# The softmax sums of the later head pairs move from TensorE to GpSimd in an attention and feed-forward kernel

## The chip, the cores and the metric

One core of a Trainium2 chip runs the whole program. The metric is the device time of one execution in microseconds; the median of several runs is compared. A "pair" below is a pair of attention heads, counted from 0 to 23.

## The reference, cut to what matters

```python
def _attn_ref(q, k, v):                      # each (4, 12, 448, 64)
    scores = scale * np.matmul(q, k.transpose(0, 1, 3, 2))
    scores = np.where(causal_mask, -1000000000.0, scores)
    scores = scores - np.max(scores, axis=-1, keepdims=True)
    attn = np.exp(scores)
    attn = attn / (np.sum(attn, axis=-1, keepdims=True) + 1e-09)
    return np.matmul(attn, v)

def _moe_ref(x, w_in, w_out):                # (1792, 768), (768, 2048), (2048, 768)
    h = x @ w_in
    g = np.maximum(0.01 * h, h)
    return g @ w_out
```

The attention's output, its heads side by side, is x. The two weight matrices come as 64-bit floats, and the kernel rebuilds 32-bit values from their words.

## The kernel before, in words

There are 4 batches of 12 heads; two heads make a pair, so each batch has 6 pairs and there are 24 in all. The 448 keys lie on partitions, in 4 chunks of 128 (the last of 64), and queries lie along the free axis; since the mask is causal, chunk c holds only the queries from 128c on, and the four chunks of a head fill 1,024 columns.

Each pair goes through these steps. Its q and k are loaded by SP (`qk_load`), TensorE turns them so that features lie on partitions and ScalarE copies the result to SBUF (`features`, L376 and L379). TensorE makes the scores and adds the mask (`scores`, L407 and L421). ScalarE copies chunk 0 and VectorE takes the maximum with the other chunks (`softmax`, L442, helper line L236), GpSimd takes the maximum over the partitions with one all-reduce per head (L450), VectorE subtracts it (L456) and ScalarE takes the exponential in place (L463). The exponentials lie in the tile `t`, of which there are three, one pair each. TensorE multiplies them by v (`products`, L474) and ScalarE copies the unnormalised output to `xu` (L480, three buffers).

`finish(u)` runs after every second pair and handles pairs u - 1 and u. It needs the sum of the exponentials over all keys, that is over all partitions and chunks. It makes them with TensorE (`sums`, L494): a matrix of ones times each chunk, four heads into one PSUM tile, 32 matmul records for the four chunks. For the batches 2 and 3 (`b >= ADDS`, with ADDS = 2, so from pair 12 on) VectorE first adds chunk 3 to chunk 2, that to chunk 1 and that to chunk 0 (three instructions per pair, helper line L236, tile `t`), and TensorE sums chunk 0 alone, 8 records. ScalarE copies the sums from PSUM (L506, `sr`), a DMA spreads the four rows over 112 partitions (`sc`), VectorE adds 1e-9 and inverts (L509, L510), a DMA stores the result to DRAM (`scr`), and four DMAs on ScalarE's queue broadcast it to `rb` (two buffers). VectorE multiplies `xu` by it, ScalarE rounds the product to the upper part of x and VectorE makes the rest (the tile `xt`).

The first layer (`layer1`, L548) takes one batch at a time: 16 blocks of 18 matmuls, with w_in in an upper and a lower part. The weights are rebuilt in 16 pieces (`weights_in`, `unpack`: L318, L320, L322, L341 on VectorE, with two copies on ScalarE each). Their staging tile is the same memory as the x of the batches 1 and 3, so these can be written only when all weights are done (batch 1), or when the first layer of batch 1 is done (batch 3). Its result goes through ScalarE (L554, two buffers) and SP to DRAM (`gd`). When attention ends, `switch` frees its memory, and the second layer (`layer2`, L735, seven products of half blocks in place of eight) has w_out rebuilt by the same kind of steps.

The order is made by a planner in Python (`Plan`). Every operation is recorded with its engine, a cost in microseconds, its tiles and a due value. `emit` then lists them: whenever an engine is free it takes, of the operations that could start within 0.1 us, the one with the lowest due value. The due value of a pair's operation is `turn(kind, u)`, that is u plus the entry of the table `LATER`; that of weight piece f is `PIECE[0] + PIECE[1] * f`; the layers' matmuls come after everything that is ready. `SAME` favours matmuls of the same layout as the one before. The order on each engine, and on SP's and ScalarE's DMA queues, is fixed by that list; on the chip each queue runs in order and waits on semaphores.

The change touches `LATER`, `PIECE`, `SAME`, `ADDS` and `finish`.

Of the kernel before, what the change touches and what calls it, by code (L numbers as in the profile page):

```python
# [8 lines left out]
F32 = mybir.dt.float32  # L9
# [3 lines left out]
ACTF = mybir.ActivationFunctionType  # L13
ALU = mybir.AluOpType
# [3 lines left out]


LATER = {  # L20
    "add": 29.11, "load": 31.13, "v": 31.53, "transpose": 32.21, "features": 48.43, "scores": -32.29,
    "chunk 0": 29.53, "max": -47.1, "all max": -30.16, "subtract": -15.76, "exp": 53.37, "products": 26.02,
    "take products": 72.72, "sums": -33.79, "take sums": -26.22, "spread": 12.66, "invert": -79.89, "store": -38.91,
    "broadcast": 59.38, "divide": -36.6, "x hi": 59.99, "x lo": 21.48,
}

EARLY = 8

PIECE = (410.28, -44.38)


SAME = 10.69


class Plan:
# [6 lines left out]

    SPLIT, SAME = 0.15, SAME

# [23 lines left out]
    def emit(self, slack, filler):  # L68
# [18 lines left out]
        def at(i):  # L87
            take = ops[i][6]
            if take is None:
                return ready[i]  # L90
            slots = self.pools[take[0]]
            return max(ready[i], min(slots)[0]) if slots else float("inf")
# [12 lines left out]
        for _ in range(n):  # L105
            t, e = min((max(free.get(e, 0.0), min(at(i) for i in c)), e) for e, c in waiting.items() if c)
            assert t < float("inf")
            i = min((i for i in waiting[e] if at(i) <= t + slack.get(e, 0.0)), 
                    key=lambda i: (ops[i][4] - (self.SAME if e == "PE" and ops[i][9] == split else 0.0), i))
            waiting[e].remove(i)  # L110
# [37 lines left out]
def attention_moe_kernel(  # L148
# [15 lines left out]
    nc = tc.nc  # L164
    w_in, w_out = w_in.bitcast(I32), w_out.bitcast(I32)
    B, H, S, D = q.shape
# [28 lines left out]
    p1 = actx.enter_context(tc.tile_pool(name="p1", bufs=1))  # L195
# [3 lines left out]
    P = Plan()  # L199
# [7 lines left out]
    def turn(kind, u):  # L207
        return u + LATER[kind]

    T = {}  # L210
# [7 lines left out]
    def pe(us, emit, r=(), w=(), prio=0.0, **kw):  # L218
        return P.op("PE", us, emit, r, w, prio, **kw)

    def act(n, emit, r=(), w=(), prio=0.0, us=0.0, **kw):
        return P.op("ACT", us or 0.066 + 0.0008 * n, emit, r, w, prio, **kw)

    def dve(n, emit, r=(), w=(), prio=0.0, rate=1.0, chain=0.0, **kw):

        return P.op("DVE", 0.07 + chain + 0.00104 * n * rate, emit, r, w, prio, **kw)

    def dma(kb, out_, in_, r=(), w=(), prio=0.0, hold=0.62, eng="SP", **kw):

        return P.op(eng, hold, lambda: (nc.sync if eng == "SP" else nc.scalar).dma_start(out=out_(), in_=in_()), r, w, prio, late=max(kb, 20) / 380.0, **kw)  # L230

    def copy(out_, in_, n, r=(), w=(), prio=0.0, **kw):
        return act(n + 55, lambda: nc.scalar.activation(out=out_(), in_=in_(), func=kw.pop("func", ACTF.Copy), **kw), r, w, prio)

    def tt(out_, a, b, op, n, r=(), w=(), prio=0.0, **kw):
        return dve(n, lambda: nc.vector.tensor_tensor(out=out_(), in0=a(), in1=b(), op=op), r, w, prio, **kw)  # L236
# [4 lines left out]
    def new(key, pool, shape, dtype, tag):  # L241
        def f():
            T[key] = pool.tile(shape, dtype, tag=tag, name="_".join(str(x) for x in key))
        return f

    def both(*fs):
        def f():
            for g in fs:
                g()
        return f  # L250
# [11 lines left out]
    ones = p1.tile([128, 32], F32, name="ones")  # L262
# [4 lines left out]
    bigs = lambda key: big[P.slot["tp", key]]  # L267
# [115 lines left out]

    order = sorted(segs)
    NTB, NM = 3, 2
    ADDS = 2
    MERGE = [lambda u: u >= 0, lambda u: u >= 99, lambda u: u >= 99]
    for tag, n, width_ in (("M", NM, S), ("MR", 1, S), ("t", NTB, 1024)):
        for i in range(n):
# [93 lines left out]
    def finish(u):  # L483

        b = u // NP
        heads = range(2 * u - 2, 2 * u + 2)
        sr, sc, rc = ("sr", 0), ("sc", 0), ("rc", 0)
        key = ("tp", ("sums", u))

        def sums():  # L490
            for c in chunks:
                qs, n, bank, col = segs[c]
                for e, g in enumerate(heads):
                    nc.tensor.matmul(out=bigs(key[1])[32 * e:32 * e + 32, qs:S], lhsT=ones, rhs=T["t", g // 2 % NTB][:, g % 2, 512 * bank + col:512 * bank + col + n],  # L494
                                     start=c == 0, stop=c == chunks[-1])


        chunks = order[:1] if b >= ADDS else order
        for w in (u - 1, u) if b >= ADDS else ():
            for c in (2, 1, 0):  # L500
                n = segs[c][1] - 128
                at = lambda c, d, w=w, n=n: T["t", w % NTB][:, :, 512 * segs[c][2] + segs[c][3] + d:512 * segs[c][2] + segs[c][3] + d + n]
                tt(lambda at=at, c=c: at(c, 128), lambda at=at, c=c: at(c, 128), lambda at=at, c=c: at(c + 1, 0), ALU.add, 2 * n,
                   (), [("t", w % NTB, e) for e in range(2)], turn("add", u), chain=0.02)
        pe(0.78 if b >= ADDS else 1.95, sums, ["ones"] + [("t", w % NTB, e) for w in (u - 1, u) for e in range(2)], [key], turn("sums", u), rows=120, cfg=4, take=key)
        act(S + 55, both(new(sr, p1, [128, S], F32, "sr"), lambda: nc.scalar.activation(out=T[sr], in_=bigs(key[1])[:, 0:S], func=ACTF.Copy)),  # L506
            [key], [sr], turn("take sums", u), give=key)
        dma(7, lambda: T[sc], lambda: T[sr][0:97:32, :].rearrange("o (p j) -> o p j", j=16), [sr], [sc], turn("spread", u), 0.68)
        dve(16, lambda: nc.vector.tensor_scalar(out=T[sc], in0=T[sc], scalar1=1e-9, scalar2=None, op0=ALU.add), (), [sc], turn("invert", u))  # L509
        dve(100, both(new(rc, p1, [CP, 16], F32, "rc"), lambda: nc.vector.reciprocal(out=T[rc], in_=T[sc])), [sc], [rc], turn("invert", u))  # L510
        scr = dp.tile([4, S], F32, name=f"scr{u}")
        dma(7, lambda: scr.rearrange("a (p j) -> (a p) j", j=16), lambda: T[rc], [rc], [("scr", u)], turn("store", u))
        slot = (b + 1) % 2
        if u % NP == 1:
            P.op("X", 0.0, new(("xt", b), xp, [128, 2 * NP, S], F32R, f"x{slot}"), w=[("x", slot)], prio=u)
        for w in (u - 1, u):
            p = w % NP
            rb, xu, xc = ("rb", w % 2), ("xu", w % 3), ("xp", b, p)
            for e in range(2):
                a = 2 * (w - u + 1) + e  # L520
                dma(158, lambda rb=rb, e=e: T[rb][64 * e:64 * e + 64, :], lambda a=a: scr[a:a + 1].to_broadcast([64, S]),
                    [("scr", u), rb], [(*rb, e)], turn("broadcast", u), 0.47, eng="ACT")
            x = lambda rb=rb: T[rb]
            tt(x, lambda xu=xu: T[xu], x, ALU.mult, S, [xu, (*rb, 0), (*rb, 1)], [rb], turn("divide", u))
            copy(lambda p=p: T["xt", b][:, p], x, S, [rb, (*rb, 0), (*rb, 1), ("x", slot)], [(*xc, "h")], turn("x hi", u))
            tt(lambda p=p: T["xt", b][:, NP + p], x, lambda p=p: T["xt", b][:, p].bitcast(F32), ALU.subtract, S, [rb, (*rb, 0), (*rb, 1), (*xc, "h"), ("x", slot)], [xc], turn("x lo", u))
# [230 lines left out]

    conv = lambda f: PIECE[0] + PIECE[1] * f
    P.op("X", 0.0, new(("stage",), xp, [128, 2 * NP * S], F32, "x0"), w=[("x", 0)], prio=FIRST)
# [6 lines left out]
    for b in range(B):  # L766
        n0 = len(P.ops)
        for u in range(NP * b, NP * b + NP):
            if u:
                qk_load(u)  # L770
            v_load(u)
            features(u)
            scores(u)
            products(u)
            if u % 2 == 1:
                finish(u)
        attention += range(n0, len(P.ops))
        if b < B - 2:
            layer1(b, lambda f: LAST + 100 * b + f)
# [39 lines left out]
```

## Time and profile before

| | |
|---|---|
| median of 3 runs | 613.22 us (612.17 to 614.36) |
| profiled execution: its own time | 613.63 us |
| profiled execution: span | 611.5 us |
| instructions | 10378 |
| HBM read, written | 61.87 MB, 20.27 MB |

The span goes from the first to the last instruction that was profiled. All times in the profile count from its start. PE is TensorE's matmul, PEld its weight load, DVE is VectorE, ACT is ScalarE, POOL is GpSimd and SP is the engine that issues most DMAs; a name with a q behind it (SPq, ACTq) is that engine's instruction queue. Matmuls are pipelined, so the busy time of PE counts overlaps once, and records of one matmul can be longer than the distance to the next.

### The profile page before, as it was taken

How to read it: one execution, taken by the hardware profiler on the slowest of the kernel's cores; microseconds unless marked ns; L12 is line 12 of the kernel's file. 1: busy time of each engine (PE TensorE's matmuls, PEld its weight loads, DVE VectorE, ACT ScalarE, POOL GpSimd, SP SyncE). 2: the span in 40 equal slices, each digit the busy share in tenths (PEclk: the TensorE clock that was granted, in tenths of full speed). 3: DMA queues.
4: the chain of work that ended last, by engine and by line, in shares of the span. 5: the costliest groups of instructions: out<-in, count | busy, mean ns of one | idle time of the engine just before them, and what ended most of it. 6: DMA issues, size and time to landing. Idle time of an engine off the chain costs nothing.

```text
span 611.5 us, 10378 instructions
## 1 busy us (share of the span) xinstructions
PE 595.1 (97%) x3864; PEld 514.4 (84%) x3864; DVE 445.6 (73%) x899; ACT 292.2 (48%) x478; POOL 81.9 (13%) x54
## 2 busy tenths in 40 slices
PE   8989899999999999999999999999999999999997
PEld 7655576689767676779999999999999999999997
DVE  4899998989678677551466899778857575767655
ACT  3778677655555645432333555545333233323331
POOL 2544323321124242220000000000000000000000
PEclk9989999999999999999999999999999999999999
DMA  8977976848375432312588864113523333333201
GB/s 197 215 174 137 189 184 185 201 127 255 118 154 136 123 86 54 92 36 89 191 284 270 285 205 133 62 46 104 155 70 120 89 116 109 101 95 94 70 31 39
DMA packets 130465, 82.89 MB, mean 136 GB/s; under 512 B 72560, under 2 KB 128368, under 8 KB 130416
## 3 DMA queue, kind: packets, MB, share of 16 engines
q1 hardware_dynamic: 126576, 76.74, 44.6%
q10 hardware_dynamic: 3840, 5.51, 3.3%
q8 instruction: 30, 0.49, 0.4%
q14 instruction: 19, 0.16, 0.1%
HBM read 61.87 MB, written 20.27 MB: 134 GB/s over the span
## 4 chain that ended last, share of the span: by engine, by line
PE 68%; DVE 15%; POOL 4%; ACT 4%; issue 3%; DMA 3%; SPq 1%; ACTq 0%; POOLq 0%; DVEq 0%
PE h L735 31%; PE h L548 28%; POOL MR L450 4%; PE S L407 4%; DVE t L456 3%; DVE M L236 3%; PE big L474 2%; DVE stage L322 2%; DVE stage L320 1%; DMA stage<-in_moe_w_in_dram 1%; PE big L376 1%; DVE wl L341 1%; DMA rb<-scr 1%; SPq L230 1%; PE big L494 1%
## 5 line engine op out<-in xcount | busy, mean ns | idle before, releaser
L548 PE MATMUL h<-xt,wh 128*128 128x448 f32 x768 | 223.1, 371 | 1.8 <-DVE t L456 1.8
L735 PE MATMUL h<-W,r 128*128 128x384 f32 x882 | 164.0, 334 | 0.1
L548 PEld LDWEIGHTS h<-xt,wh 128*128 128x128 f32 x768 | 141.2, 188 | 17.3 <-issue 4.2
L735 PEld LDWEIGHTS h<-W,r 128*128 128x128 f32 x882 | 153.7, 188 | 0.7 <-DVE r L601 0.4
L548 PE MATMUL h<-xt,wl 128*128 128x448 f32 x384 | 140.9, 367 | 0.0
L450 POOL PARTITION_ALL_REDUCE MR<-M x48 | 81.3, 1740 | 181.3 <-DVE M L236 145.5
L548 PEld LDWEIGHTS h<-xt,wl 128*128 128x128 f32 x384 | 72.1, 188 | 6.8
L600 ACT ACTIVATE r<-v 128x512 fp32r<-128x512 f32 x70 | 41.9, 599 | 71.9 <-DVE v L598 71.8
L456 DVE TENSOR_TENSOR t<-S,MR 128x64 f32<-128x64 f32 x192 | 67.8, 414 | 5.8 <-POOL MR L450 5.7
L236 DVE TENSOR_TENSOR M<-S,M 128x320 f32<-128x320 f32 x144 | 49.1, 354 | 30.3 <-ACT M L442 20.2
L601 DVE TENSOR_TENSOR r<-v,r 128x512 fp32r<-128x512 f32 x70 | 47.3, 690 | 28.3 <-ACT r L600 26.6
L554 ACT ACTIVATE h<-h 128x448 f32<-128x448 f32 x64 | 34.6, 541 | 66.3 <-PE h L548 40.1
L735 PE MATMUL h<-xw,r 128*128 128x384 f32 x294 | 61.9, 334 | 0.0
L463 ACT ACTIVATE t<-t 128x1024 f32<-128x1024 f32 x48 | 50.7, 1056 | 22.7 <-DVE t L456 20.0
L407 PE MATMUL S<-kq 64*128 64x448 f32 (+3 forms) x384 | 53.5, 413 | 3.0 <-DVE t L456 3.0
L735 PEld LDWEIGHTS h<-xw,r 128*128 128x128 f32 x294 | 51.9, 188 | 0.0
L407 PEld LDWEIGHTS S<-kq 64*128 64x128 f32 x384 | 32.7, 191 | 21.7 <-issue 10.8
L598 DVE TENSOR_TENSOR v<-A 128x512 f32<-128x512 f32 (+1 forms) x71 | 47.8, 690 | 0.0
L474 PE MATMUL big<-t,v 128*64 128x448 f32 (+3 forms) x384 | 46.0, 385 | 0.2 <-ACT kq L379 0.2
L474 PEld LDWEIGHTS big<-t,v 128*64 128x64 f32 x384 | 25.3, 137 | 20.8 <-issue 11.8
L442 ACT ACTIVATE M<-S 128x896 f32<-128x896 f32 (+1 forms) x27 | 22.1, 832 | 21.6 <-PE S L421 21.6
L600 ACT ACTIVATE r<-A 128x512 fp32r<-128x512 f32 x28 | 17.7, 632 | 30.8 <-PE h L735 30.7
(84 smaller groups left out, 517.5 us busy)
## 6 DMA issues: line engine op xcount, KB each, us to landing
gd<-h SPq DMA_DIRECT2D x64, 224.0 KB, 3.1
A<-gd SPq DMA_DIRECT2D x28, 512.0 KB, 3.9
stage<-in_moe_w_in_dram SPq DMA_DIRECT2D x16, 768.0 KB, 7.2
A<-in_moe_w_out_dram SPq DMA_DIRECT2D x16, 768.0 KB, 5.7
kraw<-in_k_dram SPq DMA_DIRECT2D x24, 224.0 KB, 5.4
qraw<-in_q_dram SPq DMA_DIRECT2D x24, 224.0 KB, 5.0
rb<-scr ACTq DMA_DIRECT2D x48, 112.0 KB, 3.0
v<-in_v_dram SPq DMA_DIRECT2D x48, 96.0 KB, 2.2
```

The source lines that it names most:

```text
L236: return dve(n, lambda: nc.vector.tensor_tensor(out=out_(), in0=a(), in1=b(), op=op), r, w, prio, **kw)
L407: nc.tensor.matmul(out=T["S", u, bank, e][:, col:col + n], lhsT=T[kq][rows, 128 * c:128 * c + 128], rhs=T[kq][rows, S + qs:2 * S], start=c ...
L450: P.op("Pool", 1.52, lambda e=e: nc.gpsimd.partition_all_reduce(T[mr][:, e], T[m][:, e], 128, ReduceOp.max), [(*m, e)], [(*mr, e)], turn(" ...
L456: i = dve(len(es) * n, lambda c=c, qs=qs, n=n, es=es: nc.vector.tensor_tensor(out=T[t][:, cut(es), at(c):at(c) + n], in0=s(c, es), in1=T[m ...
L463: act(1024 + 55, lambda e=e: nc.scalar.activation(out=T[t][:, e], in_=T[t][:, e], func=ACTF.Exp, scale=scale), (), [(*t, e)], turn("exp", u))
L474: nc.tensor.matmul(out=bigs(key[1])[64 * e:64 * e + 64, qs:S], lhsT=T[vv][:, c, e, :], rhs=T["t", u % NTB][:, e, 512 * bank + col:512 * ba ...
L548: nc.tensor.matmul(out=T[key][:, :S], lhsT=T[w, f, 1][:, 128 * c:128 * c + 128], rhs=T["xt", b][:, x, :], start=(c == 0 and j == 0), stop= ...
L554: lambda key=key, g=g: nc.scalar.activation(out=T[g], in_=T[key][:, :S], func=ACTF.Prelu, alpha=0.01)),
L598: nc.vector.tensor_tensor(out=x(), in0=get(terms[0]), in1=get(terms[1]), op=ALU.add if terms[2] > 0 else ALU.subtract)
L600: act(n, lambda: nc.scalar.activation(out=hi(), in_=x(), func=ACTF.Copy), [*rd, *hold], [(out_cell, "h")], prio)
L601: return dve(n, lambda: nc.vector.tensor_tensor(out=lo(), in0=x(), in1=hi().bitcast(F32), op=ALU.subtract), [*rd, (out_cell, "h")], [out_c ...
L735: nc.tensor.matmul(out=T[key][:, :HO], lhsT=g()[:, jj * 128:jj * 128 + 128], rhs=W[:, w * HO:(w + 1) * HO], start=(e == 0 and jj == 0 and ...
```

## The change

From finish(9) on, that is for the pairs 8 to 23, the sums are no longer made on TensorE. VectorE adds the chunks (now also for pairs 8 to 11), and GpSimd adds up the partitions of the joined chunk of each head with an all-reduce. Its result stands in every partition of a part of `t` that is free by then; four DMAs per finish, one for each head, take row 0 and spread it over 28 partitions of `sc`. The matmuls and the copy by ScalarE are left out there. Each add and each sum has the due value of its own pair, not of the second of the two. The tables of due values are replaced as a whole.

```diff
 LATER = {
-    "add": 29.11, "load": 31.13, "v": 31.53, "transpose": 32.21, "features": 48.43, "scores": -32.29,
-    "chunk 0": 29.53, "max": -47.1, "all max": -30.16, "subtract": -15.76, "exp": 53.37, "products": 26.02,
-    "take products": 72.72, "sums": -33.79, "take sums": -26.22, "spread": 12.66, "invert": -79.89, "store": -38.91,
-    "broadcast": 59.38, "divide": -36.6, "x hi": 59.99, "x lo": 21.48,
+    "add": 362.91, "load": 53.58, "v": 54.29, "transpose": 55.63, "features": 8.51, "scores": 10.32,
+    "chunk 0": -13.81, "max": 7.89, "all max": -55.51, "subtract": -33.49, "exp": 43.28, "products": 53.56,
+    "take products": 80.72, "sum all": -34.4, "sums": 31.2, "take sums": -13.17, "spread": 19.03, "invert": -30.74,
+    "store": 5.04, "broadcast": 53.24, "divide": -52.56, "x hi": 53.32, "x lo": 18.2,
 }
-PIECE = (410.28, -44.38)
+PIECE = (498.29, -44.66)
-SAME = 10.69
+SAME = 6.83
...
-    ADDS = 2
+    ADDS = 9
...
-        chunks = order[:1] if b >= ADDS else order
-        for w in (u - 1, u) if b >= ADDS else ():
+        chunks = order[:1] if u >= ADDS else order
+        for w in (u - 1, u) if u >= ADDS else ():
             for c in (2, 1, 0):
...
-                   (), [("t", w % NTB, e) for e in range(2)], turn("add", u), chain=0.02)
-        pe(0.78 if b >= ADDS else 1.95, sums, ...)
-        act(S + 55, both(new(sr, p1, [128, S], F32, "sr"), ...), [key], [sr], turn("take sums", u), give=key)
-        dma(7, lambda: T[sc], lambda: T[sr][0:97:32, :].rearrange("o (p j) -> o p j", j=16), [sr], [sc], turn("spread", u), 0.68)
-        dve(16, ... op0=ALU.add), (), [sc], turn("invert", u))
+                   (), [("t", w % NTB, e) for e in range(2)], turn("add", w), chain=0.02)
+        if u >= ADDS:
+            for w in (u - 1, u):
+                t = ("t", w % NTB)
+                for e in range(2):
+                    P.op("Pool", 3.0, lambda t=t, e=e: nc.gpsimd.partition_all_reduce(T[t][:, e, 512:512 + S], T[t][:, e, 512 - S:512], 128, ReduceOp.add),
+                         (), [(*t, e)], turn("sum all", w))
+                for e in range(2):
+                    i = 2 * (w - u + 1) + e
+                    dma(7, lambda i=i: T[sc][28 * i:28 * i + 28, :], lambda t=t, e=e: T[t][0:1, e, 512:512 + S].rearrange("o (p j) -> o p j", j=16),
+                        [(*t, e), sc], [(sc, i)], turn("spread", u), 0.68)
+        else:
+            pe(1.95, sums, ...)
+            act(S + 55, both(new(sr, p1, [128, S], F32, "sr"), ...), [key], [sr], turn("take sums", u), give=key)
+            dma(7, lambda: T[sc], lambda: T[sr][0:97:32, :].rearrange("o (p j) -> o p j", j=16), [sr], [sc], turn("spread", u), 0.68)
+        dve(16, ... op0=ALU.add), [(sc, i) for i in range(4)], [sc], turn("invert", u))
```

## Rows read from the trace of the kernel before

**Rows 1.** The page: busy time and share by engine; granted clock in 40 slices.

```profile
PE 595.1 (97%) x3864; PEld 514.4 (84%) x3864; DVE 445.6 (73%) x899; ACT 292.2 (48%) x478; POOL 81.9 (13%) x54
...
PEclk9989999999999999999999999999999999999999
```

**Rows 2.** Stretches: length, busy PE, PEld, DVE, ACT, POOL, granted clock, DMA share, GB/s.

```profile
12.00:63.00 51.00, 46.17 (x491) 30.06 (x493) 44.83 (x117) 38.92 (x58) 24.07 (x14) 0.97 0.86 191
63.00:156.00 93.00, 88.96 (x655) 69.10 (x652) 86.16 (x174) 57.68 (x80) 26.39 (x15) 1.00 0.72 184
...
164.00:271.00 107.00, 106.39 (x758) 77.55 (x758) 75.16 (x190) 54.72 (x84) 29.16 (x18) 1.00 0.40 103
...
393.00:404.00 11.00, 11.00 (x55) 10.02 (x54) 6.83 (x14) 4.62 (x12) 0.00 (x0) 1.00 0.17 63
```

**Rows 3.** The chain that ended last, in order of time: start, length, what.

```profile
176.16 1.58 PE big L494 x8
...
214.97 1.25 PE big L494 x6
...
239.90 1.74 PE big L494 x8
...
258.23 0.89 PE big L494 x8
...
271.46 129.55 PE h L548 x626
...
419.00 189.23 PE h L735 x1090
```

**Rows 4.** Timeline of TensorE from 92 us: start, length, engine, line, operation.

```profile
93.44 1.93 PE L494 MATMUL big<-t,ones 128*32 128x448 f32 x32
95.31 1.89 PE L474 MATMUL big<-t,v 128*64 128x448 f32 x14
```

**Rows 5.** Groups of VectorE by form: names, shape, count; busy us, mean ns; idle before.

```profile
L236 DVE TENSOR_TENSOR t<-t 128x640 f32<-128x640 f32 x12 | 9.8, 816 | 0.2
...
L236 DVE TENSOR_TENSOR t<-t 128x384 f32<-128x384 f32 x12 | 6.7, 557 | 0.4
...
L236 DVE TENSOR_TENSOR t<-t 128x128 f32<-128x128 f32 x12 | 5.0, 418 | 3.2 <-PE big L474 3.2
```

**Rows 6.** Lines 450 and 322: ns min/median/max, first and last start.

```profile
L450 POOL PARTITION_ALL_REDUCE MR<-M x48: 1604/1682/2392, 11.9 to 262.1; - x48
...
L322 DVE SCALAR_TENSOR_TENSOR stage<-stage x16: 948/958/1722, 24.0 to 153.2; 128x768 int32<-128x768 int32 x16
```

**Rows 7.** Timelines of VectorE and GpSimd near 117 us.

```profile
117.32 1.72 DVE L322 SCALAR_TENSOR_TENSOR stage<-stage 128x768 int32<-128x768 int32 x1 [0.76 <-ACT stage L233]
...
115.71 3.19 POOL L450 PARTITION_ALL_REDUCE MR<-M  x2 [6.89 <-DVE M L236]
```

**Rows 8.** Timeline of VectorE: the last weight piece; the fourth pair's x.

```profile
155.34 0.95 DVE L341 TENSOR_TENSOR wl<-stage,wh 128x768 fp32r<-128x768 f32 x1
...
166.03 0.63 DVE L236 TENSOR_TENSOR xt<-rb,xt 128x448 fp32r<-128x448 f32 x1 [1.34 <-ACT xt L233]
```

**Rows 9.** The first layer's matmuls (line 548) in a stretch: busy PE, PEld.

```profile
156.00:167.00 11.00, 8.99 (x43) 7.59 (x42) 1.00 0.36 121
```

**Rows 10.** Timeline of TensorE: the next batch's first matmuls.

```profile
173.58 0.64 PE L548 MATMUL h<-xt,wh 128*128 128x448 f32 x2
```

**Rows 11.** Timelines of VectorE, ScalarE's queue and SP's queue at the end of attention.

```profile
273.97 0.18 DVE L509 TENSOR_SCALAR sc<-sc 112x16 f32<-112x16 f32 x1 [3.67 <-DMA sc<-sr]
...
292.35 2.39 ACTq L230 DMA_DIRECT2D rb<-scr  x4
...
299.56 0.81 SPq L230 DMA_DIRECT2D A<-in_moe_w_out_dram  x2
```

**Rows 12.** Instructions on the tile sr: ns min/median/max, first and last start.

```profile
L506 ACT ACTIVATE sr<-big x12: 522/544/552, 28.1 to 271.6; 128x448 f32<-128x448 f32 x12
L230 SPq DMA_DIRECT2D sc<-sr x12: 570/604/677, 29.4 to 272.1; - x12
```

More of the change, by code (lines that the diff above doesn't have):

```diff
@@ L503, in finish @@
                 tt(lambda at=at, c=c: at(c, 128), lambda at=at, c=c: at(c, 128), lambda at=at, c=c: at(c + 1, 0), ALU.add, 2 * n,
-                   (), [("t", w % NTB, e) for e in range(2)], turn("add", u), chain=0.02)
-        pe(0.78 if b >= ADDS else 1.95, sums, ["ones"] + [("t", w % NTB, e) for w in (u - 1, u) for e in range(2)], [key], turn("sums", u), rows=120, cfg=4, take=key)
-        act(S + 55, both(new(sr, p1, [128, S], F32, "sr"), lambda: nc.scalar.activation(out=T[sr], in_=bigs(key[1])[:, 0:S], func=ACTF.Copy)),
-            [key], [sr], turn("take sums", u), give=key)
@@ L508, in finish @@
-        dma(7, lambda: T[sc], lambda: T[sr][0:97:32, :].rearrange("o (p j) -> o p j", j=16), [sr], [sc], turn("spread", u), 0.68)
-        dve(16, lambda: nc.vector.tensor_scalar(out=T[sc], in0=T[sc], scalar1=1e-9, scalar2=None, op0=ALU.add), (), [sc], turn("invert", u))
+                   (), [("t", w % NTB, e) for e in range(2)], turn("add", w), chain=0.02)
[10 more added lines that the diff above has]
+        else:
+            pe(1.95, sums, ["ones"] + [("t", w % NTB, e) for w in (u - 1, u) for e in range(2)], [key], turn("sums", u), rows=120, cfg=4, take=key)
+            act(S + 55, both(new(sr, p1, [128, S], F32, "sr"), lambda: nc.scalar.activation(out=T[sr], in_=bigs(key[1])[:, 0:S], func=ACTF.Copy)),
+                [key], [sr], turn("take sums", u), give=key)
+            dma(7, lambda: T[sc], lambda: T[sr][0:97:32, :].rearrange("o (p j) -> o p j", j=16), [sr], [sc], turn("spread", u), 0.68)
@@ L510, in finish @@
+        dve(16, lambda: nc.vector.tensor_scalar(out=T[sc], in0=T[sc], scalar1=1e-9, scalar2=None, op0=ALU.add), [(sc, i) for i in range(4)], [sc], turn("invert", u))
         dve(100, both(new(rc, p1, [CP, 16], F32, "rc"), lambda: nc.vector.reciprocal(out=T[rc], in_=T[sc])), [sc], [rc], turn("invert", u))
```

## The prediction

> **What bounds the kernel now.** I read the page's shares first, then the busy time by stretch, then the chain that ended last, then the rows of the operations that the diff touches. TensorE is busy for 97% of the span, VectorE for 73%, GpSimd for 13% [rows 1]; the granted clock is at full speed nearly throughout, with a dip worth 3% of the stretch from 12 to 63 us [rows 1, 2]. By stretch: up to 156 us VectorE is busy for 88% and more, and TensorE shows 4.8 and 4.0 us of idle time; from 164 to 271 us TensorE shows 0.6 us in 107, while VectorE has 32 us free and GpSimd 78 [rows 2]. The chain ends in 626 matmuls of the first layer in 129.6 us and 1090 of the second in 189.2 us, back to back [rows 3]. So from 164 us on the time is the sum of TensorE's work, and an instruction taken off TensorE there shortens the run by its length; before 156 us VectorE, which also rebuilds the weights, is the tighter engine.
>
> **TensorE: the sums that go.** The finishes of pairs 9 and 11 lose full sums of 32 matmuls. One runs from 93.44 us to the next instruction's start at 95.31: 1.87 us, two are 3.7 us [rows 4]. The six later finishes lose sums of 8 matmuls. In the chain they hold 1.58, 1.25, 1.74 and, three times, 0.89 us: 7.2 us [rows 3]. Six by the shortest would be 5.3; the 1.9 us above that are waits for VectorE's adds, which no TensorE instruction would wait for any more, though another wait may show in their place. Bounds 5.3 and 7.2; I take the middle, **6.3 us**, because TensorE has next work ready in most of this stretch.
>
> **The early sums and the new adds.** Pairs 8 to 11 get three adds each: 0.418 + 0.557 + 0.816 = 1.79 us [rows 5], four pairs 7.2 us of VectorE. Their eight GpSimd sums also stand in VectorE's way. Beside an all-reduce a VectorE instruction with two SBUF inputs took 1.72 instead of 0.96 us, a wait of 0.76 while the second of two all-reduces ran that took 3.19 together [rows 6, 7]. Eight such waits are 6.1 us; that is the upper end, the lower is none: VectorE gets 7.2 to 13.3 us more before the weights are done. What covers it: the last weight is written at 156.3 us, and TensorE still has 43 matmuls of the first layer queued until 167; the fourth pair's x that the next batch needs is written at 166.7, and its matmuls start at 173.6 [rows 8 to 10]. So x may come 6.9 us later for nothing, and TensorE would lose between 0.3 and 6.4 us after that. Against it stand the 3.7 us saved: between 3.4 gained and 2.7 lost. The middle is near nothing, and I take **0** for these two finishes.
>
> The Trainium skill (SBUF — State Buffer, section "SBUF: two separate sides") says that VectorE and GpSimd share a port pair under an exclusive lock held for the full instruction, and counts a VectorE instruction with two SBUF inputs among those that need it. The trace agrees that the two block each other, but with 0.76 us for a lock that would by the page have lasted the rest of that all-reduce, some 1.6 us. By the row the sum above stands; by the page it would be the fourth rival's.
>
> **GpSimd.** The trace has no all-reduce that adds. From below its price is the fastest maximum of the same shape, 1.60 us; the slowest took 2.39 [rows 6]. The planner's costs are 3.0 for it and 1.52 for the maximum, whose median by the trace is 1.68; scaled by that ratio the sum would last 3.3, the upper end. I take 3.0, nearer that end, because the planner's cost is the only one given for this operation. 32 of them are 96 us. In the late stretch nine pairs (18 all-reduces) take 107 us [rows 2], 23.8 us for two pairs; GpSimd needs 4 x 1.68 + 4 x 3.0 = 18.7 us of that. It stays off the path, with 5 us to spare, but no longer idle: a maximum may now queue behind a sum, and the subtraction behind it. The three buffers of exponentials are held longer, by some 6 us of sums and the transfer.
>
> **The last finish.** The sum of a pair ends 6 us (12, if both pairs' sums come last) after its adds, where it was a matmul and a copy. In the trace the last sums reach VectorE at 274.0 us, and the last four broadcasts are issued at 292.4, since they wait for buffers that the first layer frees [rows 11]. Some 18 us lie between; up to 12 us later costs nothing. If that cover is gone, the second layer's weights, whose loads start at 299.6 [rows 11], come later.
>
> **Queues and ScalarE.** Eight copies of 0.54 us leave ScalarE (4.3 us, busy 48%: nothing) [rows 1, 12]. SP gets four spreads of 0.60 us for one, 24 more issues and 14.5 us in all [rows 12]. They now wait for GpSimd; behind them on SP stand the loads of q, k and v and the stores of the first layer's result, whose two buffers TensorE's output waits for. Lower end nothing, upper end 8 x 1.8 us, each finish's three extra issues falling on a store that TensorE waits for. I take nothing: one such block of matmuls lasts 3.7 us (18 of the chain's matmuls at 0.207), longer than the extra issues, and a second buffer stands behind it.
>
> **The order.** All due times move, and every wait of the pairs with them. Bounds: the visible idle time of 9.5 us after 12 us could go, or as much be added [rows 2]. I take nothing.
>
> **Sum.** 6.3 + 0 = 6.3 us off. On the profiled execution (span 611.5, own time 613.6) that gives 605.2 and 607.3; its own time stands 0.4 above the median, so 613.2 - 6.3 = **606.9 us**.
>
> **The rivals.**
> *One: all of it counts.* The early sums lie on TensorE's path too, because layer one ends only at 167 us: 3.7 + 7.2 = 10.9 us off, 602.3. For it: TensorE is 96% busy from 63 to 156 us. Against: VectorE is as full there.
> *Two: VectorE takes the early stretch.* The upper end of its term, 2.7 us lost: 613.2 - 6.3 + 2.7 = 609.6.
> *Three, slower: GpSimd becomes the bound.* Place: the late stretch. It decides from the sum's duration at which 4 x 1.68 + 4d passes 23.8 us, d = 4.3 us. At 5.0 us each of six finishes comes 2.9 us later than the one before allows, 17.6 us at the end. The switch to the second layer waits for it; of that VectorE's idle 4.2 us between 393 and 404 us are the cover [rows 2]. The second layer starts 13.4 us later than before, 626.6. For it: GpSimd and VectorE lengthen each other (1.60 to 2.39 us). Against: 3.0 and 0.8 on top are 3.8.
> *Four, slower: a GpSimd sum holds VectorE's two-input instructions for its whole length.* Eight early sums of 3.0 us, half of it met: 12 + 7.2 - 6.9 = 12.3 lost, less 3.7 and 6.3: 615.5. This is the time by the lock that the Trainium skill's SBUF — State Buffer, "SBUF: two separate sides", describes. The 0.76 us of the trace speak against it.
> *Five: the order gives it back.* Sums queued before maxima, SP behind spreads: new waits of 6 us, two thirds of the bound above, make it 613, with as much chance above as below.
>
> **The numbers.** Forecast (604.5 to 609) 0.41, one 0.18, two 0.14, three 0.09, four 0.04, five 0.14 (0.10 within 0.3%, 0.02 and 0.02 beyond on each side). A measurement of this kernel tells 0.3%, 1.8 us, from no change. Of two, 0.02 ends within it. Faster: 0.41 + 0.18 + 0.12 + 0.02 = 0.73; same: 0.12; slower: 0.15. The range reaches from rival one's 602.0 to 613.5, which leaves out three, four, the upper side of five and a little below.
>
> **What would show it.** Right: no 8- or 32-matmul sums on TensorE after 80 us; 80 all-reduces in place of 48, the new ones near 3 us; the block of first-layer matmuls that ended at 401.0 us ending near 394.7 [rows 3]; TensorE's idle time from 164 us on still below 2 us; attention's last x near 299 us. Early step wrong if x of pairs 6 to 9 is written after 174 us and TensorE waits for it. Wrong altogether: sums of 4.3 us and more with GpSimd busy throughout from 164 us, ScalarE's results waiting for stores behind spreads on SP, or VectorE's idle time before 404 us gone and second-layer matmuls waiting for weights.

## The result and the profile after

The changed kernel took 618.67 us in the median of four executions against 612.82 us of the kernel before on the same chip: a ratio of 1.0087 (95% interval 1.0059 to 1.0114), slower by less than 1%, but clear of noise, where 606.9 us and a range of 602.0 to 613.5 us were forecast. One of the four, the one first profiled, took 1149 us with the same instructions and longer matmuls; the ratio leaves it out (the other three have a median of 618.5 us), and the profile below is that of a further run (e1) whose median is 619.05 us (ratio 1.0114, 1.0081 to 1.0146) and whose profiled execution took 619.43 us, with a span of 617.5 us.

The page of the kernel after, parts 1, 2 and 4: busy time by engine, the granted clock in 40 slices, and the shares of the chain that ended last.

```profile
PE 591.9 (96%) x3748; PEld 512.2 (83%) x3748; DVE 478.0 (77%) x911; ACT 287.9 (47%) x470; POOL 176.4 (29%) x86
...
PEclk9999999899989999999999999999999999999999
...
PE 65%; DVE 19%; POOL 5%; issue 5%; ACT 3%; DMA 2%; SPq 1%; ACTq 0%; POOLq 0%; DVEq 0%
```

Beside [rows 1], 116 matmul records are gone: the 112 of the sums (two finishes of 32, six of 8), as the change says, and four of another line (306). TensorE's busy time fell by only 3.2 us and the span rose by 6.0, so it waits more; in the chain VectorE has 19% (15% before). VectorE's busy time rose by 32.4 us. Its twelve added instructions account for 7.2 of these by [rows 5]; some 25 us are left, in which the same instructions take longer.

Windows of the kernel after: length, busy PE, PEld, DVE, ACT, POOL with their counts, granted clock, DMA share, GB/s.

```profile
12.00:63.00 51.00, 46.81 (x481) 30.23 (x483) 43.18 (x113) 37.99 (x57) 23.34 (x14) 0.97 0.86 185
63.00:156.00 93.00, 85.13 (x562) 65.22 (x558) 89.42 (x162) 52.92 (x78) 40.35 (x19) 0.98 0.72 189
100.00:120.00 20.00, 16.38 (x87) 13.53 (x87) 19.32 (x29) 9.97 (x14) 10.71 (x5) 0.91 0.65 168
164.00:180.00 16.00, 13.23 (x87) 8.63 (x85) 13.56 (x32) 6.80 (x12) 9.42 (x5) 0.89 0.34 92
164.00:271.00 107.00, 101.70 (x696) 76.40 (x695) 86.04 (x188) 50.56 (x76) 85.28 (x38) 0.98 0.38 100
393.00:404.00 11.00, 11.00 (x55) 10.00 (x54) 10.39 (x21) 6.17 (x14) 0.00 (x0) 1.00 0.16 58
```

Against [rows 2], the first and the last row show TensorE as before. Its idle time grows from 4.0 to 7.9 us in the second row's stretch, and from 0.6 to 5.3 us between 164 and 271 us, where the forecast said that it would stay below 2 us. GpSimd is idle for 21.7 us of those 107, so it is not the bound. VectorE is busy for 86 us of them, 11 more than before. The granted clock also falls in two new places, from 100 to 120 us and from 164 to 180 us. TensorE has two levels, 2.4 and 1.2 GHz, and a mean of 0.91 over 20 us is 3.6 us at the lower one. In both stretches TensorE was short of work first (16.38 busy of 20, 13.23 of 16): from 112 to 114 us it was busy for 0.67 us at a granted clock of 1.00, and from 116 to 118 the clock was 0.50; from 170 to 172 it was busy for 0.45 us, and from 174 to 176 the clock was 0.50.

The chain of waits of the kernel after, around the end of the first layer (start, length, what).

```profile
399.96 9.51 PE h L559 x46
409.46 10.58 PE h L746 x61
```

The first layer ends at 409.5 us. In the kernel before its last matmul ended at 403.7; the block of [rows 3] ends at 401.0 because the chain leaves TensorE there. So it ends 5.8 us later, nearly the whole loss, where the forecast wanted that block to end 6.3 us earlier. The second layer follows it without a gap.

### The profile page after: what moved, and what is told of

The parts are those of the page before. It is cut to its first block, busy times and chain, and to the rows that moved or that the text cites. A ratio compares the mean times of both kernels' runs of the same rounds, so it can differ in the third digit from the quotient of the medians.

```text
span 1147.4 us, 10264 instructions
## 1 busy us (share of the span) xinstructions
PE 1142.1 (100%) x3748; PEld 814.0 (71%) x3748; DVE 474.9 (41%) x911; ACT 283.6 (25%) x470; POOL 176.3 (15%) x86
## 4 chain that ended last, share of the span: by engine, by line
PE 99%; DVE 0%; ACT 0%; issue 0%
PE h L559 41%; PE h L746 36%; PE S L407 8%; PE big L474 8%; PE big L376 3%; PE big L494 1%; PE S L421 1%; PE big L306 1%; DVE place L276 0%; DVE ob L760 0%; ACT C L757 0%; PE big L278 0%; DVE row L279 0%; DVE warmb L270 0%; DVE ones L239 0%
## 5 line engine op out<-in xcount | busy, mean ns | idle before, releaser
L559 PE MATMUL h<-xt,wh 128*128 128x448 f32 x768 | 394.9, 615 | 0.0
L746 PE MATMUL h<-W,r 128*128 128x384 f32 x882 | 323.0, 556 | 0.0
L746 PEld LDWEIGHTS h<-W,r 128*128 128x128 f32 x882 | 263.2, 300 | 46.0 <-issue 31.3
L559 PEld LDWEIGHTS h<-xt,wh 128*128 128x128 f32 x768 | 220.1, 292 | 83.3 <-issue 69.2
L559 PE MATMUL h<-xt,wl 128*128 128x448 f32 x384 | 235.1, 612 | 0.0
L559 PEld LDWEIGHTS h<-xt,wl 128*128 128x128 f32 x384 | 112.6, 293 | 41.6 <-issue 35.2
L746 PE MATMUL h<-xw,r 128*128 128x384 f32 x294 | 117.2, 558 | 0.6 <-ACT C L757 0.6
L565 ACT ACTIVATE h<-h 128x448 f32<-128x448 f32 x64 | 34.9, 545 | 303.1 <-issue 162.4
L509 POOL PARTITION_ALL_REDUCE t<-t x32 | 95.0, 3014 | 55.4 <-DVE t L236 28.1
L407 PE MATMUL S<-kq 64*128 64x448 f32 (+3 forms) x384 | 94.9, 655 | 0.0
L474 PE MATMUL big<-t,v 128*64 128x448 f32 (+3 forms) x384 | 92.3, 672 | 0.0
```

What stands on the lines that cost most here:

```text
L407: nc.tensor.matmul(out=T["S", u, bank, e][:, col:col + n], lhsT=T[kq][rows, 128 * c:128 * c + 128], rhs=T[kq][rows, S + qs:2 * S], start=c ...
L474: nc.tensor.matmul(out=bigs(key[1])[64 * e:64 * e + 64, qs:S], lhsT=T[vv][:, c, e, :], rhs=T["t", u % NTB][:, e, 512 * bank + col:512 * ba ...
L509: P.op("Pool", 3.0, lambda t=t, e=e: nc.gpsimd.partition_all_reduce(T[t][:, e, 512:512 + S], T[t][:, e, 512 - S:512], 128, ReduceOp.add), ...
L559: nc.tensor.matmul(out=T[key][:, :S], lhsT=T[w, f, 1][:, 128 * c:128 * c + 128], rhs=T["xt", b][:, x, :], start=(c == 0 and j == 0), stop= ...
L746: nc.tensor.matmul(out=T[key][:, :HO], lhsT=g()[:, jj * 128:jj * 128 + 128], rhs=W[:, w * HO:(w + 1) * HO], start=(e == 0 and jj == 0 and ...
```

## Where the time went

The line of the new all-reduce in the kernel after: ns min/median/max, first and last start.

```profile
L509 POOL PARTITION_ALL_REDUCE t<-t x32: 2873/2952/3432, 104.0 to 294.8; - x32
```

A sum lasts 2.95 us, beside the 1.68 us of a maximum in [rows 6]. The forecast took 3.0 us. Its length was not the error.

Groups of VectorE by form, of the kernel after: names, shape, count; busy us, mean ns; idle before.

```profile
L322 DVE SCALAR_TENSOR_TENSOR stage<-stage 128x768 int32<-128x768 int32 x16 | 19.3, 1204 | 0.7 <-ACT stage L233 0.3
...
L236 DVE TENSOR_TENSOR t<-t 128x384 f32<-128x384 f32 x16 | 16.6, 1035 | 0.5
L236 DVE TENSOR_TENSOR t<-t 128x640 f32<-128x640 f32 x16 | 15.5, 969 | 0.6
L236 DVE TENSOR_TENSOR t<-t 128x128 f32<-128x128 f32 x16 | 6.0, 378 | 2.4 <-PE big L474 2.4
```

The weight step of line 322 has a median of 0.958 us in both kernels [rows 6]; its mean was 1.04 and is now 1.20. Of the adds, which took 0.816, 0.557 and 0.418 us [rows 5], the one of 384 columns now has nearly double its time and is the longest, although the one of 640 has more to do: what was added is waiting, not work.

Two instructions of VectorE, and what GpSimd did beside them, in the timelines of the kernel after (start, length, engine, line, operation; in brackets the idle time before).

```profile
111.10 2.19 DVE L318 TENSOR_SCALAR stage<-stage 128x768 int32<-128x768 int32 x1
...
119.27 2.67 DVE L322 SCALAR_TENSOR_TENSOR stage<-stage 128x768 int32<-128x768 int32 x1 [0.27 <-ACT stage L233]
```

```profile
110.83 3.06 POOL L509 PARTITION_ALL_REDUCE t<-t  x1
...
119.17 5.82 POOL L509 PARTITION_ALL_REDUCE t<-t  x2 [5.28 <-DVE t L236]
```

Line 322 starts 0.10 us after the first of two sums and ends 2.77 us after the sum began. Less its own 0.96 us it was held for 1.71, until 1.81 us into the sum: neither the 0.76 us of [rows 7] nor the whole 2.91 us. Line 318, which has one input in SBUF, is held in the same way: it takes 0.55 us when alone (at 121.62 us in the kernel before), and here it ends 2.46 us after the sum before that began, which puts the end of its hold at 1.91 us. The subtractions of line 456, which read one input from PSUM, show no hold: the longest of 192 took 0.62 us.

Counted in this way, as an instruction's length less its length alone, the eight sums of the pairs 8 to 11 held eight instructions, by 0.58, 1.64, 1.71, 0.65, 1.66, 1.87, 0.43 and 0.89 us: 9.4 us. All 32 sums come to some 22 us. The holds beside the maxima rose as well, from 4 to 9 us, but they stay as high in e5 below, which loses nothing.

So the weights come late. The first layer's matmuls with the lower part of the weights in the kernel after (busy us, mean ns; idle time of TensorE before them, and what ended it), and three moments in the timelines of VectorE and of TensorE:

```profile
L559 PE MATMUL h<-xt,wl 128*128 128x448 f32 x384 | 142.1, 370 | 3.8 <-DVE wl L341 3.8
```

```profile
161.41 0.95 DVE L341 TENSOR_TENSOR wl<-stage,wh 128x768 fp32r<-128x768 f32 x1
...
174.51 0.64 DVE L236 TENSOR_TENSOR xt<-rb,xt 128x448 fp32r<-128x448 f32 x1
```

```profile
178.67 0.64 PE L559 MATMUL h<-xt,wh 128*128 128x448 f32 x2
```

In the kernel before these matmuls waited for no weight piece at all. Now TensorE waits three times for the lower part of one, 3.8 us in all, 2.54 of them before 115.21 us. The last piece is written at 162.4 us (156.3 before), the fourth pair's x at 175.2 (166.7) [rows 8]. The matmuls at 178.67 (173.58 before [rows 10]) are the last three of the first batch, since 285 of its 288 come before them. The next batch starts behind them, at 179.35 us (175.30): 4.0 us later, though 3.7 us of sums have left TensorE by then.

## The experiments

Theories, by the letters that the expectations use. **A**: TensorE is short of work and its clock falls. **B**: the replaced order costs the time. **C**: GpSimd's sums hold VectorE's instructions whose inputs all lie in SBUF. **D**: the time that GpSimd needs for a sum makes what waits for it late. **E**: the adds, the spreads or the order that came with the sums cost it.

**e1, the change again.** No edit; for its profile.

> The changed kernel, unedited, for a profile at full clock. All theories: 618.5 us (617.5 to 619.5). Theory A, TensorE runs short of work and its clock falls: mean granted clock 0.989 to 0.994, at least two dips of 3 us or more to the lower level where the kernel before had one, TensorE's idle time outside the dips up by 5 us or more. Theory B, the replaced order delays x: the first matmul of the second batch's first layer starts after 180 us (before 173.6). Theory C, GpSimd's sums hold up VectorE: VectorE's instructions with two SBUF inputs that meet a sum last 1.5 us longer and more, together over 15 us.

619.05 us. The loss stands, with the profile shown above. C's sign is there (some 22 us beside sums, line 318's among them), and so is A's, two new falls of the clock; B's is not, since the second batch starts at 179.35 us, not after 180.

**e2, the new order alone, and e3, the sums in the old order.** Is it B?

```diff
 # e2: the kernel before with the new LATER, PIECE, SAME
 # e3: the changed kernel with the old ones
+    "sum all": -9.05,
```

> The kernel before with the changed tables of due values; the sums stay on TensorE as before. Theory B, the order is what costs: 616 us or more. Theories A and C, it is the sums on GpSimd: within 2 us of the kernel before, 611 to 615.

> The changed kernel with the due values of the kernel before; the new sums get -9.05, 21 behind the maximum, as in the change. Theory B: 608 us or less, the order was at fault. Theories A and C: 617 us or more, since the sums themselves hold up VectorE or starve TensorE whatever the order.

e2 took 614.8 us (1.0040, 1.0014 to 1.0066) and e3 631.9 us (1.0318, 1.0287 to 1.0349). With the sums on TensorE the new order costs 2.6 us (the kernel before took 612.2 beside it); with them on GpSimd it saves 13 against the old one. B falls: the order relieves what the sums do.

**e4, from pair 12 on.** Only the pairs whose weights are done by then should be left.

```diff
-    ADDS = 9
+    ADDS = 13
```

> The changed kernel with the new sums from pair 12 on only; pairs 8 to 11 have their full sums on TensorE as before and no adds. If the loss lies in the early stretch (VectorE full of weights): 610 us or less. If it lies in the later one: 616 us or more.

618.33 us (1.0089, 1.0055 to 1.0123), no gain, which by the expectation puts the loss into the later stretch. But the timelines of VectorE and GpSimd of this kernel, and its window from 180 to 271 us, show another order:

```profile
156.70 2.59 DVE L320 SCALAR_TENSOR_TENSOR stage<-stage 128x768 int32<-128x768 int32 x1
159.39 2.75 DVE L322 SCALAR_TENSOR_TENSOR stage<-stage 128x768 int32<-128x768 int32 x1
...
163.72 0.95 DVE L341 TENSOR_TENSOR wl<-stage,wh 128x768 fp32r<-128x768 f32 x1
```

```profile
156.36 5.89 POOL L509 PARTITION_ALL_REDUCE t<-t  x2 [10.06 <-DVE t L236]
```

```profile
180.00:271.00 91.00, 84.14 (x568) 63.45 (x567) 72.72 (x145) 40.43 (x60) 70.33 (x30) 0.98 0.36 95
```

The planner made the order anew, and put the first two sums beside the rebuilding of the last weight pieces; the last was written at 164.7 us. TensorE's idle time from 180 to 271 us is 6.9 us here and 2.5 in the change, with the same late sums. One edit changed two things, so this run tells nothing apart. From here on the operation was replaced and the order kept.

**e5, e6, e7: something else in the place of each sum, order kept.** One memset of the same tile (no reading, short), six memsets (no reading, as long as a sum), a maximum (reading, shorter). The sums themselves are left out.

```diff
-partition_all_reduce(T[t][:, e, 512:512 + S], T[t][:, e, 512 - S:512], 128, ReduceOp.add)
+nc.gpsimd.memset(T[t][:, e, 512:512 + S], 100.0)                           # e5
+[nc.gpsimd.memset(T[t][:, e, 512:512 + S], 100.0) for _ in range(6)]       # e6
+partition_all_reduce(T[t][:, e, 512:512 + S], T[t][:, e, 512 - S:512], 128, ReduceOp.max)  # e7
```

> The changed kernel with every one of the 32 sums on GpSimd replaced by one memset of the same output; order, adds, spreads and waits are the same (the sums are left out). Theory C, the sums hold up VectorE's two-input instructions: 606 to 610 us, VectorE's instructions with two SBUF inputs back to their own length beside them. Theory D, the sums come late on GpSimd and what waits for them is late: the same, 606 to 610. Theory E, it is the adds, the four spreads and the order, not the operation on GpSimd: 616 us or more.

> The same with six memsets in place of each sum, so that GpSimd is busy for about as long as with the sum (estimate from a memset of 128 columns at 0.2 us: 2.5 to 3.5 us) but reads nothing (the sums are left out). Theory C: 606 to 611 us, since no instruction of VectorE is held. Theory D, GpSimd's time itself: 616 us or more.

> The changed kernel with a maximum in place of each sum, same order (the sums are left out). A maximum lasts 1.7 us and held VectorE 0.8 to 0.9 us, a sum lasts 3.0 and held it 1.8 to 1.9. Theories C and D: between the change and the run with one memset, 610 to 615 us. Theory E: 616 us or more.

e5 took 603.6 us (0.9837, 0.9790 to 0.9884), e6 606.3 (nine executions, a tenth took 613.9; 0.9900, 0.9868 to 0.9933), e7 606.3 (0.9890, 0.9838 to 0.9942). All three beat the kernel before, though each has the adds, the spreads and the order of the change: E falls. e5 is 2 us below what was expected of it and e7 4 us. The instruction that is held at 119.27 us in the kernel after, in the timelines of VectorE and GpSimd of e5:

```profile
115.04 0.96 DVE L322 SCALAR_TENSOR_TENSOR stage<-stage 128x768 int32<-128x768 int32 x1 [0.25 <-ACT stage L233]
```

```profile
114.91 0.89 POOL L509 MEMSET t<- 128x448 f32 x2 [6.24 <-DVE t L236]
```

and of e6:

```profile
117.15 0.96 DVE L322 SCALAR_TENSOR_TENSOR stage<-stage 128x768 int32<-128x768 int32 x1 [0.26 <-ACT stage L233]
```

```profile
117.01 6.78 POOL L509 MEMSET t<- 128x448 f32 x12 [3.31 <-DVE t L236]
```

and in e7, with the row of its maxima in line 509:

```profile
116.15 1.66 DVE L322 SCALAR_TENSOR_TENSOR stage<-stage 128x768 int32<-128x768 int32 x1 [0.26 <-ACT stage L233]
```

```profile
L509 POOL PARTITION_ALL_REDUCE t<-t x32: 1602/1681/2162, 102.9 to 281.7; - x32
```

Beside memsets it takes its 0.96 us, beside a maximum 1.66, beside a sum 2.67. In e6 GpSimd is at work for 3.39 us per head, longer than with a sum, and this instruction is not held; that costs 2 to 3 us against e5. D can have about that much. The sums cost 15.4 (619.0 less 603.6), so C has some 12. A is a consequence: in e5's profile the granted clock is 1.00 between 63 and 300 us, where TensorE waits less (in e14, the same kernel again, it is 0.99, with one fall there). Over the whole kernel the page gives VectorE 478.0 us busy in the kernel after, 457.6 in e5 and 453.6 in e6: 20 to 24 us of holds.

The cost does not go by the length of a hold alone. With maxima VectorE is busy for 463.0 us, a quarter of the way from e5 to the change, and the time is 2.7 us above e5, a sixth of the sums' cost: short holds are mostly covered. One rival is not tested by itself: without the sums x has other values. That e5 and e7, which divide by very different numbers (100 and a maximum), are both fast speaks against it.

**e9, e10: which sums?** Memsets for the sums of pairs 8 to 11 alone (e9), or of pairs 12 to 23 alone (e10); the order is that of the change.

```diff
+(nc.gpsimd.memset(...) if u < 13 else partition_all_reduce(...))     # e9
+(nc.gpsimd.memset(...) if u >= 13 else partition_all_reduce(...))    # e10
```

> The changed kernel with the eight sums of pairs 8 to 11 replaced by one memset each, same order (these sums are left out); pairs 12 to 23 keep theirs. All 32 left out gave 603.6 us, none 619. Theory C1, the holds cost time only where VectorE is full of weights: 606 us or less. Theory C2, they cost in both stretches, and by the ends of the first layer's batches (11 of 15 us lost by the end of the first batch) mostly early: 608 to 612. Theory C3, mostly late: 614 or more.

> The reverse: the 24 sums of pairs 12 to 23 replaced by one memset each, those of pairs 8 to 11 kept. C1: 616 us or more. C2: 610 to 615. C3: 608 or less.

e9 took 610.4 us (0.9958, 0.9939 to 0.9977), e10 611.3 (0.9978, 0.9957 to 1.0000): both as C2 has it.

**e13 to e16: the same kernels again.** A reading of the windows stood in the way: in e9's profile the first layer's matmuls lay further apart than in e10's, 4 to 5 us over the layer, which would have changed the division. No edits: e13 is the kernel before, e14 is e5, e15 is e9, e16 is e10.

> The kernel before, a second profile. Execution (the spacing of the first layer's matmuls varies from execution to execution): 292 or 298 of them between 320 and 380 us, either. Kernel (it belongs to the program): 292 or 293 again, and a time near 612.7.

> The change with each sum replaced by one memset, a second profile. Execution: 292 or 298 matmuls of the first layer between 320 and 380 us, and executions about 4.8 us apart, 603 to 608. Kernel: 298 again, 603.6 again.

> The change with the sums of pairs 8 to 11 replaced by memsets, a second profile. Execution: 292 or 298 matmuls between 320 and 380 us, median near 610.4. Kernel: 292 again; then 4.8 of the 6.8 us between this kernel and the one without sums are the spacing, and the late sums cost 2 to 3 us, not 7.8.

> The change with the sums of pairs 12 to 23 replaced by memsets, a second profile. Execution: 292 or 298 matmuls between 320 and 380 us, median near 611.3. Kernel: 297 or 298 again; then the early sums cost 7.7 us at equal spacing, as before.

The window from 320 to 380 us (columns as above), of e9 and, the same kernel, e15:

```profile
320.00:380.00 60.00, 60.00 (x292) 54.49 (x292) 49.66 (x79) 29.06 (x53) 0.00 (x0) 1.00 0.75 246
```

```profile
320.00:380.00 60.00, 60.00 (x298) 55.61 (x297) 48.76 (x76) 28.07 (x52) 0.00 (x0) 1.00 0.74 239
```

and of e10 and, the same kernel, e16:

```profile
320.00:380.00 60.00, 60.00 (x297) 55.61 (x297) 50.68 (x80) 29.86 (x53) 0.00 (x0) 1.00 0.75 251
```

```profile
320.00:380.00 60.00, 60.00 (x292) 54.50 (x291) 48.86 (x75) 29.08 (x51) 0.00 (x0) 1.00 0.78 256
```

292 matmuls became 298, and 297 became 292: the spacing belongs to the single execution, so medians of several executions may be compared, and spans of two profiles only to within 5 us. The kernel before, run beside each set of experiments, had medians of 612.1 to 612.8 us, so sets may be put together. e13 took 612.4 us (0.9998, 0.9979 to 1.0016), e14 604.8 (0.9882, 0.9845 to 0.9919), e15 609.4 (0.9949, 0.9925 to 0.9973), e16 613.2 (1.0018, 0.9999 to 1.0037).

The medians over both sets of each kernel: no sums 604.1 (8 executions), the late ones alone 609.9 (19), the early ones alone 612.5 (20), all of them 618.7 (7, the change's own included). The eight early sums thus cost 8.4 us (612.5 - 604.1) or 8.8 (618.7 - 609.9), the 24 late ones 5.8 or 6.2, whichever is taken first; together they are the 14.6 us. Resampling the executions leaves 1 to 2 us of doubt on each side of these four. Per sum an early one costs some four times as much as a late one. The windows show where. The kernel before, before and after the last weight piece:

```profile
100.00:165.00 65.00, 61.58 (x407) 50.81 (x404) 57.66 (x106) 40.24 (x57) 14.20 (x8) 1.00 0.62 173
...
180.00:271.00 91.00, 90.47 (x644) 66.58 (x642) 64.10 (x166) 46.28 (x68) 25.75 (x16) 1.00 0.35 94
```

Without sums, in the order of the change (e5):

```profile
100.00:165.00 65.00, 61.00 (x367) 49.36 (x365) 59.51 (x106) 38.60 (x57) 14.39 (x15) 1.00 0.63 180
...
180.00:271.00 91.00, 90.54 (x622) 69.25 (x621) 67.85 (x164) 44.71 (x67) 34.20 (x34) 1.00 0.34 93
```

With the early sums alone (e10):

```profile
100.00:165.00 65.00, 57.03 (x318) 45.91 (x313) 63.10 (x96) 33.09 (x49) 29.91 (x13) 0.97 0.58 168
...
180.00:271.00 91.00, 90.43 (x621) 69.36 (x619) 66.47 (x161) 45.65 (x67) 34.12 (x34) 1.00 0.40 104
```

With the late sums alone (e9):

```profile
100.00:165.00 65.00, 60.59 (x367) 49.48 (x365) 58.59 (x103) 38.67 (x56) 13.77 (x14) 1.00 0.64 182
...
180.00:271.00 91.00, 88.11 (x608) 66.43 (x608) 70.04 (x158) 44.08 (x64) 75.97 (x34) 1.00 0.34 93
```

Early, against e5: VectorE does 96 instructions where it did 106, in 3.6 us more; it is busy for 63 of 65 us, TensorE loses 4.0 us of busy time and the clock falls to 0.97. From 100 to 180 us TensorE is idle for 10.0 us in e10 and 8.9 in e16, against 4.2 and 4.3 in e5 and e14: 5.2 more. The granted clock over these 80 us is 0.96 and 0.94 instead of 1.00, which is 3.2 and 4.8 us. An estimate from these rows is thus 5.2 of waiting and some 4 of clock, near the 8.4 to 8.8 measured; no run separates the two.

Late: VectorE has 21 us free in 91 and TensorE is yet idle for 2.9 us instead of 0.5. Free time on VectorE does not cover a hold there, because each engine takes its instructions in order, and behind the held one stand steps that others wait for. The longest of these waits, in the timelines of GpSimd, VectorE, ScalarE and TensorE of e9:

```profile
196.18 5.96 POOL L509 PARTITION_ALL_REDUCE t<-t  x2 [3.38 <-issue]
```

```profile
194.29 5.12 DVE L236 TENSOR_TENSOR t<-t 128x128 f32<-128x128 f32 x6
```

```profile
201.81 0.58 ACT L233 ACTIVATE xt<-rb 128x448 fp32r<-128x448 f32 x1 [1.03 <-DVE rb L236]
202.29 0.53 ACT L480 ACTIVATE xu<-big 128x448 f32<-128x448 f32 x1
```

```profile
202.87 0.60 PE L376 MATMUL big<-ident,qraw 112*128 112x112 f32 x4 [1.11 <-ACT xu L480]
```

The same in e5, VectorE, ScalarE and TensorE:

```profile
191.50 3.39 DVE L236 TENSOR_TENSOR t<-t 128x128 f32<-128x128 f32 x6
```

```profile
198.17 0.58 ACT L233 ACTIVATE xt<-rb 128x448 fp32r<-128x448 f32 x1 [0.18 <-DVE rb L236]
```

```profile
199.23 0.60 PE L376 MATMUL big<-ident,qraw 112*128 112x112 f32 x4 [0.26 <-ACT xu L480]
```

A sum holds one of the six adds, so they take 5.12 us instead of 3.39. VectorE's multiplication into `rb` comes later, ScalarE waits 1.03 us for it instead of 0.18, and its copy to `xu`, which TensorE's line 376 waits for, stands behind. Part of the late cost can be D: in e6, with no sum to hold VectorE, TensorE is idle for 1.7 us of the same 91. No run separates the two there.

**e8, e11, e12: sums on GpSimd only where VectorE has no weights to rebuild.** Based on the kernel before and its order; from pair 18 (e8), 16 (e11) or 14 (e12) on, TensorE's sums as before up to there.

```diff
+    "sum all": -9.05,
-    ADDS = 2
+    ADDS, ALL = 13, 19        # e11: 17, e12: 15
...
+        if u >= ALL:
+            ...               # GpSimd's sums, as in the change
+        else:
+            pe(0.78 if u >= ADDS else 1.95, sums, ...)
```

> The kernel before with its own due values, and the sums on GpSimd for pairs 18 to 23 only (three finishes), where VectorE has no weights to rebuild. Theory C: the holds meet free time of VectorE there; three sums of 0.9 to 1.7 us leave TensorE, 609 to 612 us against 612.2. If the holds cost as much there as elsewhere: 613 us or more.

> As the run with the sums on GpSimd for pairs 18 to 23 (608.5 us), with the due values of the kernel before, but from pair 16 on: four finishes. If the holds go on meeting free time of VectorE: 607 to 608.5. If one more finish already puts them on the path: 610 or more.

> The same from pair 14 on: five finishes. Free time of VectorE: 606 to 608. Holds on the path: 611 or more.

608.5 us (0.9927, 0.9902 to 0.9952), 607.9 (0.9913, 0.9878 to 0.9947) and 609.9 (0.9961, 0.9933 to 0.9990). All three beat both kernels; the best two cannot be told apart. e12 lies between the two answers expected of it. The planner made these orders anew as well, so they show that the placing pays, and not what a single hold costs. In e8 the same two windows are close to the kernel before:

```profile
100.00:165.00 65.00, 62.92 (x408) 51.80 (x407) 56.87 (x106) 40.86 (x59) 14.80 (x8) 1.00 0.63 176
...
180.00:271.00 91.00, 90.22 (x629) 68.70 (x626) 66.13 (x161) 44.30 (x66) 52.99 (x26) 1.00 0.35 93
```

TensorE is idle for 0.8 us of the second, though GpSimd is busy for 53 us of it. Here the matmuls that left TensorE show as time saved.

## Why the prediction was wrong

- **The early sums: the step that failed.** It priced a sum's hold by one row, "a wait of 0.76 while the second of two all-reduces ran", as eight such waits of 6.1 us at most, and took 0 for the two finishes, with 2.7 us as the worst. That row was of a maximum. A sum held the same line 322 for 1.71 us, and the single-input line 318 too; the eight early sums held VectorE for 9.4 us, and they cost 8.4 to 8.8 us of time. The place was wrong as well. The forecast looked for the loss at the next batch's x, and took the first batch's last matmuls [rows 10] for the next batch's first. Its own sign came in by half: x was written after 174 us, but 4.2 us before the batch began, and hardly any of TensorE's waiting was for it. TensorE waited for the weight pieces, 3.8 us, and its clock fell.
- **Rival four** had the mechanism: a hold of the whole length, 615.5 us. The rule that it went by, that of the Trainium skill (SBUF — State Buffer, section "SBUF: two separate sides"), holds in its direction; by the profile, whose spans of GpSimd are rough, the measured hold was 1.8 to 1.9 us of 2.95, not the full instruction. It came nearest to 618.7 us and had a chance of 0.04. For the eight early sums it gave 12 us of holds; 9.4 were measured. What it left out were the late sums.
- **GpSimd "stays off the path, with 5 us to spare".** It is idle for 21.7 of 107 us, and rival three did not come; e6 leaves it some 2 to 3 us. But its sums stand in VectorE's way there too: the late ones cost 5.8 to 6.2 us, for which nothing was put down. VectorE's 32 us free between 164 and 271 us are no cover for a held step on which others wait.
- **TensorE's sums and the adds.** With the holds gone, the change gains 8.3 us (612.4 in e13, 604.1 without sums). By the forecast's own terms it would be 9.7 without holds: 6.3 late, 3.7 early, less the 0.3 that its adds alone would cost. So the terms were right in kind and 1.4 us large; whether the sums, the adds or the order took that, no run separates. Of the "three times, 0.89" in the chain, [rows 3] has one; the other two were assumed.
- **The clock** was given no term. The new stretches at 0.91 and 0.89 follow TensorE's waits; they are worth 1.8 us each (0.09 x 20, 0.11 x 16), about 3.6 us of the 14.6. No run separates them from the waits.
- **Right:** the sum's duration (3.0 forecast, 2.95 measured); ScalarE's copies and SP's spreads, at nothing, in so far as e5 has them all and still gains 8.3; the last finish, whose cover held: w_out's loads start at 310.84 us instead of 299.56 [rows 11], and the second layer still begins right after the first.
- **The order,** taken as nothing with 9.5 us either way: 2.6 us of loss in the kernel before, 13 of gain under the sums. It has no single price.

Sum: 8.3 gained, 14.6 lost, 6.3 us slower. The forecast had 10.0 gained on TensorE (6.3 and 3.7) and 3.7 given back by the early adds and holds, 6.3 us faster; that the two results are equal in size is chance.

## What to carry to other kernels

When work moves to an engine that stands in another's way, price the hold by the same kind of operation, or take the other instruction's whole length as the bound, with a real chance; a hold seen beside a shorter operation is no upper end. Ask of the held engine not whether it has time to spare but whether the held step feeds the bottleneck: the same sums cost 1.1 us each beside weights that TensorE waits for, 0.25 us each later, and among the last pairs they gained. To find the cost of one operation in a planned kernel, replace it with another in the same place; an edit that lets the planner order anew tests two things at once.

## What was not expected of the hardware

- How long GpSimd holds VectorE goes by what it does: a maximum over the partitions of a 128x448 tile for 0.8 to 0.9 of its 1.68 us, a sum for 1.8 to 1.9 of its 2.95, and later where GpSimd's instruction was itself longer. A memset did not hold line 322; the int32 instruction of line 318, with a single SBUF input, lost up to 0.2 us beside memsets (0.77 us at 137.20 us in e6) and was held by sums (2.19 us instead of 0.55).
- Line 318 can be held a second time, near a sum's end: in the kernel after it started at 106.73 us, 2.71 us into a sum of 3.43, and took 1.13 us. A two-input instruction that started 2.48 us into a sum, line 320 at 124.43 us, took its 0.96.
- The first layer's matmuls go at one of two spacings, 60/298 = 0.201 or 60/292 = 0.205 us, throughout one execution and at a granted clock of 1.00; the same program shows both. The cause stays open.
- The execution of 1149 us stays unexplained too. Its profile holds no record of the granted clock, so a lower clock is not excluded.
